# Attention followed by two mixers on one core: input splits moved to the values' copies, both X operands of a head in one tile, fewer transfers to fill it

## The chip, the cores and the metric

The kernel runs on one core of one Trainium2 chip. TensorE (PE in the profile) multiplies, VectorE (DVE), ScalarE (ACT) and GpSimd (POOL) work on elements, and SyncE (SP) issues most of the DMA transfers. Each engine works its own queue of instructions in order. The metric is the device time of one execution in microseconds (us). Three runs of the kernel before took 878.94, 878.44 and 873.46 us, a median of 878.44 us.

## The reference

Three stages run one after the other on 4 sequences of 576 positions and 512 channels:

```python
scores = scale * q @ k^T                       # 4 x 8 heads, 576 x 64
bias = -(cum[:, None] - cum[None, :])          # cum: running sum of max(s, 0)
scores = where(causal, -1e9, scores + min(bias, 0))
attn = softmax(scores) ; x = attn @ v          # heads side by side: 576 x 512
xk, xr = mu * x + (1 - mu) * x_prev            # x_prev: one position earlier
k = max(xk @ w_k, 0) ; y = sigmoid(xr @ w_r) * (k * k @ w_v)
u = y + (max(y^T @ w_tok1, 0) @ w_tok2)^T      # mixes positions
out = u + max(u @ w_ch1, 0) @ w_ch2            # mixes channels
```

All of it is in 32-bit floats. The kernel keeps that precision by writing most operands as a sum hi + lo of two values of TensorE's faster format (fp32r) and multiplying hi by hi, hi by lo and lo by hi.

## The kernel before

**Attention.** The 8 heads of sequence 0 are computed first, with plain 32-bit products (`early` for the first 256 positions, `late` for the rest). The 24 heads of sequences 1 to 3 follow, and each is called a *visit*, 0 to 23. A visit's scores are computed in row blocks j = 0 to 3 of 128 rows. The last 64 rows of an even visit and of the odd one behind it share a block j = 4, which stands in the even visit, so that this block already needs the operands of the odd visit. `scores` (L303) multiplies for each block: L317 takes the tile X1 (4 rows with the bias, and hi of q and k on partitions 64 to 127), L318 the tile X2 (lo of q with hi of k on partitions 0 to 63, hi of q with lo of k on 64 to 127). VectorE finds the row maximum (L288), ScalarE exponentiates (L299), GpSimd divides by the sum (L302). `transposes` turns the block, and `values` (L475) multiplies by V in two column parts c = 0 and 1 per visit. At its end ScalarE copies half of the result out of the accumulator into the tile `tmp` (L503, 48 copies in all), and VectorE adds the other half to it (L506).

**Where X1 and X2 come from.** q and k of two heads (an even and an odd visit) are split in four *splits*, 48 in all and numbered s = 0 to 47. `split` (L235): ScalarE rounds the raw piece to hi (L75, tile PB), GpSimd subtracts to get lo (L242), SyncE writes both to the buffer `hl_d` in the chip's memory (L243) and loads the raw piece of split s + 3 (L232). The place for hi and lo is double, so split s needs the write of split s - 2 to have landed. Splits 4m to 4m + 3 belong to visits 2m and 2m + 1. `place` (L270) then fills X1 and X2 of one visit with four transfers: the bias rows (L276) and three pieces of `hl_d` (L277 to L279). There are two sets of X tiles, so the fill of visit i waits until the last product of visit i - 2 is done (for even visits: of the block j = 4 of visit i - 2). `load_v` (L252) fetches V of two heads into the tile VS with three transfers, `split_v` makes hi and lo of it.

**The mixers.** Products of the first mixer (`h`, `r`, `vd`, all L108) of the sequence before are interleaved with the attention, the second mixer comes after it.

**What sets the order.** The code is recorded in blocks with places (`with at(...)`), and a scheduler with its own model of the durations makes the fixed order of each engine's queue from them. `split_at` gives the splits their places; since a split depends on nothing but its raw piece and the double place, the scheduler is free to draw it forward. All the transfers spoken of here stand in SyncE's one queue: a transfer that waits there holds up those behind it.

## Time and profile before

| | |
|---|---|
| runs | 878.94, 878.44, 873.46 us |
| profiled execution, its own time | 876.96 us |
| its span, first to last instruction | 874.9 us |
| mean granted clock of TensorE | 0.984 |
| busy share | PE 97%, DVE 55%, ACT 52%, POOL 39% |
| moved by DMA | 108.34 MB |

The span is what the trace shows; 2.06 us of the execution lie outside it. The busy share is an average over the span. A table by stretches of time tells which engine limits a stretch, a table of waits tells what ended the idle time of an engine, and the granted clock, 1.00 or 0.50 of full speed, tells how fast TensorE worked in a stretch: 1.00 is its level of 2.4 GHz, 0.50 that of 1.2 GHz.

### The profile page before, as it was taken

What the parts mean: (1) busy time and instruction counts of PE and PEld (TensorE: products, weight loads), DVE (VectorE), ACT (ScalarE), POOL (GpSimd) and SP (SyncE); (2) the same over time, 40 slices, a digit from 0 to 9 for tenths busy, and PEclk for the clock granted to TensorE, in tenths of its full rate; (3) what the DMA queues carried; (4) which work ended last, traced back from release to release, by engine and by line L of the source; (5) the groups of instructions that cost most, each with busy time, mean ns of one, the idle gap of its engine ahead of it and who ended that gap; (6) DMA issues with size and microseconds to landing.
All of it is one profiled execution on the core that took longest, in us unless ns stands there. A gap on an engine that the chain in (4) does not pass through costs nothing. (4 is left out here: it accounts for less than half of the span.)

```text
span 874.9 us, 17429 instructions
## 1 busy us (share of the span) xinstructions
PE 847.9 (97%) x6125; PEld 794.3 (91%) x6125; DVE 484.6 (55%) x1351; ACT 453.5 (52%) x1256; POOL 339.6 (39%) x600
## 2 busy tenths in 40 slices
PE   7999999989799999999999999999999999999998
PEld 5756767989699999999999889999999999999998
DVE  4877775565879566985469756961331222222221
ACT  3988866865785756868377864840310211211210
POOL 3664766765785534645257844720000000000000
PEclk7989999999999999999999999999999999999999
DMA  7953598689963344431234645562022112112100
GB/s 186 255 154 92 168 254 233 183 244 248 239 183 86 91 113 114 99 97 37 82 97 137 219 141 194 181 197 90 10 85 60 41 34 73 37 37 70 41 25 25
DMA packets 88023, 108.34 MB, mean 124 GB/s; under 512 B 11152, under 2 KB 71568, under 8 KB 87936
## 3 DMA queue, kind: packets, MB, share of 16 engines
q1 hardware_dynamic: 81408, 91.56, 37.6%
q0 software_dynamic: 4576, 15.08, 5.4%
q8 instruction: 48, 0.79, 0.4%
q10 hardware_dynamic: 1952, 0.60, 0.4%
q14 instruction: 39, 0.32, 0.1%
HBM read 77.74 MB, written 28.90 MB: 122 GB/s over the span
## 5 line engine op out<-in xcount | busy, mean ns | idle before, releaser
L862 ACT ACTIVATE HID<-c 128x256 fp32r<-128x256 f32 (+1 forms) x96 | 39.3, 409 | 220.7 <-PE c L108 220.6
L108 PE MATMUL vd<-KK,WV 128*128 128x256 f32 (+1 forms) x768 | 123.4, 304 | 0.1
L108 PEld LDWEIGHTS vd<-KK,WV 128*128 128x128 f32 x768 | 109.3, 192 | 3.4 <-issue 1.1
L302 POOL TENSOR_SCALAR P<-P,sum 128x128 f32<-128x128 f32 (+4 forms) x148 | 92.9, 631 | 40.6 <-DVE sum L301 34.8
L108 PE MATMUL h<-XK,WK 128*128 128x320 f32 (+1 forms) x672 | 106.1, 303 | 2.0 <-ACT k L533 1.7
L108 PE MATMUL c<-HID,WV 128*128 128x256 f32 (+1 forms) x768 | 104.8, 291 | 0.0
L108 PE MATMUL c<-U,WK 128*128 128x256 f32 (+1 forms) x768 | 103.2, 291 | 1.3 <-DVE HID L863 1.3
L108 PEld LDWEIGHTS c<-HID,WV 128*128 128x128 f32 x768 | 100.6, 188 | 0.0
L108 PEld LDWEIGHTS c<-U,WK 128*128 128x128 f32 x768 | 98.6, 188 | 1.6 <-DVE HID L863 1.6
L299 ACT ACTIVATE P<-P,mx 128x128 f32<-128x128 f32 (+4 forms) x148 | 86.6, 586 | 23.7 <-DVE mx L288 22.8
L108 PEld LDWEIGHTS h<-XK,WK 128*128 128x128 f32 x672 | 94.2, 190 | 3.8 <-ACT k L533 2.2
L863 DVE SCALAR_TENSOR_TENSOR HID<-c,HID 128x256 fp32r<-128x256 f32 (+1 forms) x96 | 43.8, 456 | 81.1 <-ACT HID L862 81.0
L288 DVE CUSTOM_DVE_ANT_0 P<-s,maskc 128x128 f32<-128x128 f32 (+4 forms) x148 | 72.1, 498 | 28.2 <-PE t L442 15.1
L927 DVE TENSOR_TENSOR ut<-c,ut 128x256 f32<-128x256 f32 (+1 forms) x32 | 14.6, 458 | 119.0 <-PE c L108 108.1
L108 PE MATMUL r<-XR,WR 128*128 128x320 f32 (+1 forms) x384 | 63.3, 305 | 0.0
L536 POOL TENSOR_TENSOR KK<-k,KK 128x256 fp32r<-128x256 f32 (+1 forms) x64 | 56.9, 893 | 14.8 <-ACT k L535 13.7
L300 POOL TENSOR_SCALAR sum<-sum 128x1 f32<-128x1 f32 (+1 forms) x148 | 31.6, 214 | 77.4 <-ACT P L299 70.1
L108 PEld LDWEIGHTS r<-XR,WR 128*128 128x128 f32 x384 | 54.1, 190 | 1.3 <-ACT k L535 0.2
L108 PE MATMUL c<-HID,WR 128*128 128x256 f32 (+1 forms) x384 | 54.8, 291 | 0.0
L108 PE MATMUL c<-U,C1A 128*128 128x256 f32 (+1 forms) x384 | 52.8, 296 | 0.0
L318 PE MATMUL s<-X 128*128 128x128 f32 (+3 forms) x144 | 45.8, 323 | 6.2 <-DMA X<-hl_d 6.2
L108 PEld LDWEIGHTS c<-U,C1A 128*128 128x128 f32 x384 | 51.5, 190 | 0.2 <-ACT U L912 0.2
(130 smaller groups left out, 1661.4 us busy)
## 6 DMA issues: line engine op xcount, KB each, us to landing
X<-hl_d SPq DMA_DIRECT2D x72, 288.0 KB
hl_d<-PB SPq DMA_DIRECT2D x48, 288.0 KB
raw<-in_moe_w_ch_dram POOLq DMA_DIRECT2D x48, 256.0 KB, 3.4
PB<-in_qk_dram SPq DMA_DIRECT2D x48, 144.0 KB
yt<-y_d SPq DMA_DIRECT2D x16, 288.0 KB
u_d<-yt SPq DMA_DIRECT2D x16, 288.0 KB
raw<-in_moe_w_k_dram SPq DMA_DIRECT2D x8, 512.0 KB
raw<-in_moe_w_v_dram SPq DMA_DIRECT2D x16, 256.0 KB
```

The lines of the kernel that those rows point to most:

```text
L108: nc.tensor.matmul(ps, a, b, start=first and i == 0, stop=last and i == n - 1)
L288: nc.vector.tensor_tensor_reduce(out=P[0:m, c0:c1], in0=ps[0:m, 0:c1 - c0], in1=mask[0:m], scale=-scale, scalar=3.0e38 if x == 0 else mx[0 ...
L299: nc.scalar.activation(out=P[0:m, 0:w], in_=P[0:m, 0:w], func=AF.Exp, bias=mx[0:m, x:x + 1], scale=-1.0, accum_out=sm[0:m, 0:1])
L300: nc.gpsimd.tensor_scalar(out=sm[0:m, 0:1], in0=sm[0:m, 0:1], scalar1=1e-9, scalar2=1.0, op0=ALU.add, op1=ALU.mult)
L302: nc.gpsimd.tensor_scalar(out=P[0:m, 0:w], in0=P[0:m, 0:w], scalar1=sm[0:m, 1:2], scalar2=1.0, op0=ALU.mult, op1=ALU.mult)
L318: nc.tensor.matmul(ps[0:n, 0:c1 - c0], x2[:, 0, a:a + n], x2[:, 1, c0:c1], start=False, stop=True)
L536: nc.gpsimd.tensor_tensor(out=kk[:, 1, m, 0:n], in0=t[:, 0:n], in1=f32(kk[:, 0, m, 0:n]), op=ALU.subtract)
L862: nc.scalar.activation(out=hi, in_=ps, func=AF.Relu)
L863: nc.vector.scalar_tensor_tensor(out=lo, in0=ps, scalar=0.0, in1=f32(hi), op0=ALU.max, op1=ALU.subtract)
L927: nc.vector.tensor_tensor(out=t, in0=ps, in1=t, op=ALU.add)
```

## The change

1. X1 and X2 of a visit become one tile XX of four rows of 576: rows 2 and 3 are X1, rows 1 and 0 are X2. The order of hi and lo in `hl_d` is changed, so that all of partitions 64 to 127 comes in one transfer and the rest of X2 in another: three transfers with the bias rows instead of four, of the same bytes in all. The heads of sequence 0 use the same two tiles, two heads in each, and `late_load` loads two heads together. The rows of zeros of the second tile are written when visit 0 begins, no longer before.
2. Splits 0 to 10 keep places of their own in the table, items 13 to 23. Each later split s = 2i + c + 11 is recorded in `values(i, c)`, behind the copy and the sum, and the copy goes into the split's own place in PB instead of `tmp`. So a split from 11 on can't be finished before that copy and sum, and the copy can't begin before the write of split s - 2 has landed.
3. The last 64 positions of V, which are wanted twice, come in one transfer instead of two, and the load of V moves from block 1 to block 3 of the odd visit.

```diff
-    def x_tile(slot, dtype=F32):
-        return qk_p.tile([128, 2 * S], dtype, tag=f"X{slot}", name=f"X{slot}").rearrange("p (t s) -> p t s", t=2)
+    XX = {}
+
+    def x_tile(x, dtype=F32):
+        return qk_p.tile([128, 4, S], dtype, tag=f"XX{x}", name=f"XX{x}")
+
+    def x_pair(x):
+        XX[x] = x_tile(x, F32R)
+        nc.gpsimd.memset(f32(XX[x][0:64, 2:4]), 0.0)
...
     def xs(i):
-        return X1[i % 2], X2[i % 2]
+        x = XX[i % 2]
+        return x[:, 2:4], (x[:, 1], x[:, 0])
...
     RAW = 3
+    LEAD = 11
+
+    def split_place(s):
+        o = RAW * S // 2 + s % 2 * S
+        return stage()[:, o:o + S]
...
-        o = RAW * S // 2 + s % 2 * S
-        e = stage()[:, o:o + S].rearrange("p (t s) -> p t s", t=2)
-        copy("A", e[:, 1].bitcast(F32R), t)
-        nc.gpsimd.tensor_tensor(out=e[:, 0], in0=t, in1=e[:, 1], op=ALU.subtract)
-        nc.sync.dma_start(out=hl_d[g:g + 2, :, 2 * x:2 * x + 2, c0:c1].rearrange("h d t s -> (h d) t s"), in_=e)
+        e = split_place(s).rearrange("p (t s) -> p t s", t=2)
+        hi, lo = (e[:, 0], e[:, 1]) if x == 0 else (e[:, 1], e[:, 0])
+        copy("A", hi.bitcast(F32R), t)
+        nc.gpsimd.tensor_tensor(out=lo, in0=t, in1=hi, op=ALU.subtract)
+        o = 1 - x
+        nc.sync.dma_start(out=hl_d[g:g + 2, :, o:o + 3:2, c0:c1].rearrange("h d t s -> (h d) t s"), in_=e)
         if s + RAW < 2 * len(visits):
             load(s + RAW)
...
-        for r in (0, TAIL):
-            nc.sync.dma_start(out=VS[r:r + TAIL, n], in_=v[b, 128 * n:S, h * D:(h + 2) * D])
+        tail = v[b, 128 * n:S, h * D:(h + 2) * D]
+        twice = bass.AP(tensor=tail.tensor, offset=tail.offset, ap=[[0, 2], *tail.ap])
+        nc.sync.dma_start(out=VS[:, n], in_=twice)
...
-        if i < 2:
-            X2[i] = x_tile(2 + i, F32R)
-        x1, x2 = xs(i)
-        nc.sync.dma_start(out=f32(x1[0:4]), in_=ext_d[g])
-        nc.sync.dma_start(out=f32(x1[64:128]), in_=t[:, 1:4:2])
-        nc.sync.dma_start(out=f32(x2[0:64]), in_=t[:, 0:4:3])
-        nc.sync.dma_start(out=f32(x2[64:128]), in_=t[:, 1:3])
+        both = bass.AP(tensor=t.tensor, offset=t.offset, ap=[[4 * S, D], [S, 2], [1, 2 * S]])
+        x = f32(XX[i % 2])
+        nc.sync.dma_start(out=x[0:4, 2:4], in_=ext_d[g])
+        nc.sync.dma_start(out=x[64:128].rearrange("p (x t) s -> p x (t s)", x=2), in_=both)
+        nc.sync.dma_start(out=x[0:64, 0:2], in_=t[:, 2:4])
...
                 nc.tensor.matmul(ps[0:n, 0:c1 - c0], x1[:, 0, a:a + n], x1[:, 1, c0:c1], start=True, stop=False)
-                nc.tensor.matmul(ps[0:n, 0:c1 - c0], x2[:, 0, a:a + n], x2[:, 1, c0:c1], start=False, stop=True)
+                nc.tensor.matmul(ps[0:n, 0:c1 - c0], x2[0][:, a:a + n], x2[1][:, c0:c1], start=False, stop=True)
...
-        x = late_x[h] = x_tile(h % 4)
+        if h % 2 == 0:
+            late_x[h + 1] = x_tile(h // 2 % 2)
+        x = late_x[h] = late_x[h + 1 - h % 2][:, h % 2 * 2:h % 2 * 2 + 2]
         nc.sync.dma_start(out=x[0:D], in_=qk[h])
         nc.sync.dma_start(out=x[D:D + 4], in_=ext_d[h])
...
-        tmp = v_p.tile([128, CM], F32, tag="tmp", name="tmp")
+        s = 2 * i + c + LEAD
+        tmp = split_place(s)
         nc.scalar.activation(out=tmp[a, 0:n], in_=ps[z, :], func=AF.Copy)
         cols = [(0, n, base)] if c == 0 or e else [(0, TAIL, S - TAIL), (TAIL, n, base)]
         for c0, c1, q in cols:
             nc.vector.tensor_tensor(out=x[a, 1 + q:1 + q + c1 - c0], in0=ps[a, c0:c1], in1=tmp[a, c0:c1], op=ALU.add)
+        if s < 2 * len(visits):
+            split(s)
...
-    for y in range(2 * len(visits)):
-        n = 15 + y if y < 4 else N1 + PER // 4 * (y // 4) + 2 * (y % 4) - (13 if y < 8 else 14)
+    for y in range(LEAD):
+        n = 24 - LEAD + y
         split_at.setdefault(n, []).append(y)
...
-            if j == 2 and 0 < h and h + 3 < H:
+            if j == 2 and h % 2 == 0 and 0 < h and h + 3 < H:
                 with at(N0 + n):
+                    late_load(h + 2)
                     late_load(h + 3)
...
-                    for x in range(2):
-                        X1[x] = x_tile(x, F32R)
-                        nc.gpsimd.memset(f32(X1[x][0:64]), 0.0)
+                    x_pair(0)
             if h == H - 1 and j == 2:
                 with at(N0 + n):
...
@@ -691,13 +707,16 @@
         js = visits[i][1]
         if j == 0 and i + 1 < len(visits):
             with at(N0 + n):
+                if i == 0:
+                    x_pair(1)
                 place(i + 1)
         pieces(n)
         if i % 2 and j == 1 and i + 1 < len(visits):
             with at(N0 + n + 0.2):
                 split_v(i + 1)
-                if i + 3 < len(visits):
-                    load_v(i + 3)
+        if i % 2 and j == 3 and i + 3 < len(visits):
+            with at(N0 + n + 0.2):
+                load_v(i + 3)
...
+        both = x_tile(1)
         for y in (4, 6):
-            t = x_tile(y // 2).rearrange("p t s -> p (t s)")
-            early_at.append((t, y, 2))
+            early_at.append((both[:, y - 4:y - 2].rearrange("p t s -> p (t s)"), y, 2))
             early_load(y)
```

Three places of the queues, before and now. X0 and X2 are the tiles of even visits before, XX0 that now; PB is the place of the splits, hl_d the buffer in memory, y_d takes the first mixer's output.

SyncE at the fill of visit 8 (its transfers end each piece), before:

```order
L565 DMA y_d_75<-e_2572 128x320
L243 DMA hl_d_74<-PB_1219 128x2x288
L232 DMA PB_1219<-in_qk_dram 128x288
L276 DMA X0_1477<-ext_d_73 4x1152
L277 DMA X0_1477<-hl_d_74 64x2x576
L278 DMA X2_1582<-hl_d_74 64x2x576
L279 DMA X2_1582<-hl_d_74 64x1152
```

and now:

```order
L582 DMA y_d_75<-e_2731 128x320
L289 DMA XX0_1479<-ext_d_73 4x1152
L256 DMA hl_d_74<-PB_1212 256x1x288
L244 DMA PB_1212<-in_qk_dram 128x288
L290 DMA XX0_1479<-hl_d_74 64x2x1152
L291 DMA XX0_1479<-hl_d_74 64x1152
```

The write of a split (it is split 20) and a raw load now stand between the bias rows and the two large pieces of the fill; before they stood ahead of it.

SyncE at the fill of visit 10, before:

```order
L257 DMA VS_101<-in_v_dram 64x128 x2
L243 DMA hl_d_74<-PB_1219 128x2x288
L232 DMA PB_1219<-in_qk_dram 128x288
L243 DMA hl_d_74<-PB_1219 128x2x288
L232 DMA PB_1219<-in_qk_dram 128x288
L243 DMA hl_d_74<-PB_1219 128x2x288
L232 DMA PB_1219<-in_qk_dram 128x288
L276 DMA X0_1477<-ext_d_73 4x1152
L277 DMA X0_1477<-hl_d_74 64x2x576
L278 DMA X2_1582<-hl_d_74 64x2x576
L279 DMA X2_1582<-hl_d_74 64x1152
```

and now:

```order
L271 DMA VS_101<-in_v_dram 128x1x128
L256 DMA hl_d_74<-PB_1212 256x1x288
L244 DMA PB_1212<-in_qk_dram 128x288
L256 DMA hl_d_74<-PB_1212 256x1x288
L244 DMA PB_1212<-in_qk_dram 128x288
L289 DMA XX0_1479<-ext_d_73 4x1152
L290 DMA XX0_1479<-hl_d_74 64x2x1152
L291 DMA XX0_1479<-hl_d_74 64x1152
```

Before, the writes ahead of the fill were splits of much later visits. Now the last write ahead of it is split 23, which is a part of visits 10 and 11 themselves, so that the fill needs it.

ScalarE around the copies of the values of visit 5, both parts, and visit 6, part 0 (tmp or PB from pv), before:

```order
L503 ACTIVATE tmp_2606<-pv_2601 64x256
L75 ACTIVATE PB_1219<-PB_1219 128x288
L451 ACTIVATE PF_2722<-t_2703 128x384
L299 ACTIVATE P4_2807,sum_2821<-P4_2807,mx_2808 128x576
L523 ACTIVATE XK_677<-t_2954 128x256
L299 ACTIVATE P0_2857,sum_2863<-P0_2857,mx_2858 128x128
L299 ACTIVATE P1_2900,sum_2906<-P1_2900,mx_2901 128x256
L75 ACTIVATE PB_1219<-PB_1219 128x288
L470 ACTIVATE PT0_1814<-t_2761 128x3x128
L299 ACTIVATE P2_2924,sum_2930<-P2_2924,mx_2925 128x384
L503 ACTIVATE tmp_2671<-pv_2661 64x320
```

and now:

```order
L518 ACTIVATE PB_1212<-pv_2643 64x320
L311 ACTIVATE P0_2838,sum_2844<-P0_2838,mx_2839 128x128
L484 ACTIVATE PT0_1818<-t_2744 128x3x128
L311 ACTIVATE P1_2874,sum_2880<-P1_2874,mx_2875 128x256
L540 ACTIVATE XK_674<-t_2931 128x256
L484 ACTIVATE PT0_1818<-t_2761 128x4x128
L75 ACTIVATE PB_1212<-PB_1212 128x288
L311 ACTIVATE P2_2901,sum_2907<-P2_2901,mx_2902 128x384
L75 ACTIVATE PB_1212<-PB_1212 128x288
L311 ACTIVATE P3_2938,sum_2944<-P3_2938,mx_2939 128x512
L518 ACTIVATE PB_1212<-pv_2707 64x256
```

Now the copy of part 1 of visit 5 goes into the place of split 22 and the next one, of part 0 of visit 6, into that of split 23. The two roundings (L75) between them are those of split 23 (the first: its hi lies where that copy does not write) and of split 22.

## Rows read from the trace of the kernel before

**Rows 1.** The page's part 1: busy us (share of the span), xinstructions.

```profile
PE 847.9 (97%) x6125; PEld 794.3 (91%) x6125; DVE 484.6 (55%) x1351; ACT 453.5 (52%) x1256; POOL 339.6 (39%) x600
```

**Rows 2.** Stretches A:B, us, busy of each engine, then PEclk, DMA share, GB/s.

```profile
126.00:256.00 130.00, 118.17 (x801) 107.62 (x801) 86.02 (x290) 93.58 (x267) 90.80 (x166) 0.97 0.83 225
256.00:430.00 174.00, 173.93 (x1320) 170.77 (x1320) 125.89 (x386) 119.37 (x324) 86.20 (x166) 1.00 0.33 86
```

**Rows 3.** Waits of PE, 126 to 260 us: us in total, times, longest.

```profile
PE s L318 <- DMA X<-hl_d: 6.2, 4, 1.8
...
PE s L317 <- DVE mx L288: 1.4, 4, 0.5
```

**Rows 4.** Timeline of PE: start, us, instruction, [idle before <-what ended it].

```profile
146.39 0.45 PE L318 MATMUL s<-X 128*128 128x128 f32 x1 [1.45 <-DMA X<-hl_d]
...
193.89 0.30 PE L318 MATMUL s<-X 128*128 128x128 f32 x1 [1.81 <-DMA X<-hl_d]
...
217.41 0.30 PE L318 MATMUL s<-X 128*128 128x128 f32 x1 [1.32 <-DMA X<-hl_d]
...
235.04 0.33 PE L318 MATMUL s<-X 128*128 128x128 f32 x1 [1.65 <-DMA X<-hl_d]
```

**Rows 5.** Stretches as in Rows 2, behind the first of these waits.

```profile
146.40:149.70 3.30, 3.30 (x14) 3.26 (x15) 1.33 (x5) 2.11 (x5) 3.10 (x6) 0.50 1.11 257
```

**Rows 6.** DMA issues by line, part 6 of the page: xcount, KB of each.

```profile
X<-hl_d SPq DMA_DIRECT2D x72, 288.0 KB
hl_d<-PB SPq DMA_DIRECT2D x48, 288.0 KB
...
PB<-in_qk_dram SPq DMA_DIRECT2D x48, 144.0 KB
```

**Rows 7.** Timeline of SP's queue: first issue of five fills (visits 2, 6, 8, 10; a late one).

```profile
139.49 0.27 SPq L276 DMA_DIRECT2D X<-ext_d  x1
...
186.21 0.35 SPq L276 DMA_DIRECT2D X<-ext_d  x1
...
209.91 0.34 SPq L276 DMA_DIRECT2D X<-ext_d  x1
...
228.11 0.30 SPq L276 DMA_DIRECT2D X<-ext_d  x1
...
355.71 0.27 SPq L276 DMA_DIRECT2D X<-ext_d  x1
```

**Rows 8.** Stretches as in Rows 2, at the fill that begins at 355.71 us.

```profile
360.50:361.50 1.00, 1.00 (x9) 0.99 (x8) 0.75 (x3) 0.95 (x3) 0.83 (x3) 1.00 0.47 97
361.50:362.00 0.50, 0.50 (x5) 0.42 (x4) 0.50 (x1) 0.50 (x2) 0.50 (x2) 1.00 0.00 0
```

**Rows 9.** Tile PB, 126 to 256 us (busy ACT, POOL); then its writes as a line.

```profile
126.00:256.00 130.00, 16.61 (x38) 31.07 (x38) 0.97 0.83 225
...
L243 SPq DMA_DIRECT2D hl_d<-PB x48: 359/375/535, 94.7 to 256.1; - x48
```

**Rows 10.** Waits of ACT, 85 to 260 us: us in total, times, longest.

```profile
ACT PB L75 <- DMA hl_d<-PB: 19.2, 16, 3.1
```

**Rows 11.** Lines L503 and L506, 126 to 256 us; L503, 205 to 245 us.

```profile
L503 ACT ACTIVATE tmp<-pv x19: 375/383/437, 143.8 to 252.4; 64x256 f32<-64x256 f32 x10, 64x320 f32<-64x320 f32 x9
...
L506 DVE TENSOR_TENSOR xt<-pv,tmp x24: 197/408/498, 145.4 to 253.6; 64x256 f32<-64x256 f32 x15, 64x64 f32<-64x64 f32 x5, 64x320 f32<-64x320 f32 x4
...
L503 ACT ACTIVATE tmp<-pv x8: 376/404/435, 206.0 to 239.3; 64x320 f32<-64x320 f32 x4, 64x256 f32<-64x256 f32 x4
```

**Rows 12.** Timeline: a write of a split, and the ACT rounding that waited for it.

```profile
130.18 0.41 SPq L243 DMA_DIRECT2D hl_d<-PB  x1
...
134.48 0.45 ACT L75 ACTIVATE PB<-PB 128x288 fp32r<-128x288 f32 x1 [2.64 <-DMA hl_d<-PB]
```

**Rows 13.** Timeline of ACT: the copy of visit 6, part 0.

```profile
222.19 0.38 ACT L503 ACTIVATE tmp<-pv 64x256 f32<-64x256 f32 x1
```

**Rows 14.** Zero rows of X, both tiles, ns min/median/max.

```profile
L680 POOL MEMSET X<- x2: 1061/1062/1064, 87.6 to 100.3; 64x1152 f32 x2
```

## The prediction

> **What bounds the kernel now.** I read the page's part 1 first: TensorE is busy for 847.9 us, 97% of the span [rows 1], so only its idle time and the time it spends at half clock can be won; the change takes no product away. Then the stretches [rows 2]: from 126 to 256 us, visits 1 to 11, PE works 118.17 of 130 us, so 11.83 us are idle, the granted clock is 0.97 in the mean, and the DMA engines are 0.83 busy at 225 GB/s. From 256 to 430 us PE is idle for 0.07 us and the DMA share is 0.33. So everything that this change can win lies before 256 us. Third, what PE waited for there [rows 3]: 6.2 us in four waits for the tiles that fills bring, 1.4 us for row maxima; the rest are gaps that no wait explains, and I leave them. Fourth, the four waits themselves [rows 4], always in front of L318, the second product of a block, so X2 was late and X1 was not. Last, the clock: right behind the first of them the granted clock is 0.50, the level of 1.2 GHz, for about 3.3 us [rows 5], after PE had stood still for 1.45 us. The mean of 0.97 over 130 us lacks 0.03 x 130 = 3.9 us of full clock; as rounded it may be 3.3 to 4.6, so I take two such stretches, behind the waits of visits 2 and 6, which cost half of their length each, 3.4 us together (estimate from rows 2 and 5).
>
> **Why the fills are late.** A fill's time is the end of the wait [rows 4] less its first issue [rows 7]: 6.90, 7.68, 7.50 and 6.93 us for visits 2, 6, 8 and 10. PE was ready (start less wait) 5.45, 5.87, 6.18 and 5.28 us after that issue. A lone fill, issued at 355.71 us [rows 7], ends near 361.3: in 360.5 to 361.5 the DMA share is 0.47, afterwards 0 [rows 8]. So 5.6 us for 864 KB (three times 288, rows 6), bias rows apart. The fills lose 1.3 to 2.1 us to other transfers, largely splits: 38 of the 48 are made between 126 and 256 us [rows 9], 432 KB each [rows 6].
>
> **Part by part, against 876.96 us.**
>
> Paced splits. The copies that carry them are 19 in that stretch [rows 11], so some 19 splits move behind 256 us, 19 x 432 KB = 8.2 MB of the 29 MB that 225 GB/s make in 130 us; about 160 GB/s are left. Behind 256 us they cost ScalarE 0.44 us each (16.61/38) and GpSimd 0.82 (31.07/38) [rows 9], where these engines are busy for 119 and 86 of 174 us [rows 2]: nothing, with at most 19 x 0.82 us of GpSimd's work as price were that slack gone.
>
> Visit 2: a fill of 5.6 us against a PE that is ready at 5.45 leaves a wait of 0.15 for 1.45: -1.30 (bounds -1.45 and 0). Visit 6: 5.6 against 5.87, wait gone: -1.81 (bounds -1.81 and 0).
>
> Visit 8: a split's write and a raw load now stand between the bias rows and the large pieces (SyncE's rows in the change). They add 432 KB at 225 GB/s, 1.9 us, and two issues of about 0.4 [rows 12]: 5.6 + 1.9 + 0.8 = 8.3 us against 6.18, a wait of 2.1 for 1.32: +0.8. Bounds: -1.32 if they hide beside the fill, +3 if the write must itself wait for GpSimd there.
>
> Visit 10: the fill now needs split 23, whose hi and lo come behind the copy of visit 6, part 0, at 222.19 us [rows 13]. From there: copy 0.38, sum 0.41 [rows 11], rounding beside them, GpSimd 0.82, issue and landing 3.9 (the write issued at 130.18 ended the wait of the rounding at 134.48, less 0.41 of it as issue: rows 12). That is 0.38 + 0.41 + 0.82 + 0.41 + 3.9 = 5.9 us, so 228.1, which is when this fill was issued before. The large pieces take 5.3 to 5.6 behind it and PE is ready at 233.39: a wait of 0 if no queue waits, of 5 if ScalarE or GpSimd are behind by one other piece of work each. I take the middle, 2.5 for 1.65: +0.9 (bounds -1.65, +3.4).
>
> Clock: without the waits of visits 2 and 6 nothing lets the clock fall there: -3.4. Bounds -3.4 and 0: other waits may fell it.
>
> ScalarE's new wait. A copy into a split's place needs the write of the split before last. Behind the copy stand the exponentials of the next block, for which GpSimd, the transposes and at last PE wait. Before, only roundings waited for such writes, 19.2 us in 16 waits, 1.2 in the mean and 3.1 at most [rows 10], and PE did not care. The copies lie 4.75 us apart (eight from 206.0 to 239.3, rows 11), so the write two back was begun 9.5 us earlier; its chain of 5.9 us ends well before that. I take one of these waits reaching PE, +1.2 (bounds 0, and 8 x 3.1 if all copies between visits 6 and 10 meet the longest).
>
> At nothing, together: one issue less for a fill, whose end its bytes set (at most -0.6 each); one issue less for V and its load two blocks later, since its VS is wanted a visit on; `tmp`'s buffers; the rounding that waits for VectorE's sum, 0.41 us [rows 11], in three of four splits, hidden by the 4.75 us; two heads of sequence 0 in one tile, whose loads run ahead of their use; the second tile's zeros, 1.06 us on GpSimd [rows 14], now at the start of visit 0 (at most +1.1, if its division is what PE waits for).
>
> Merged pieces: all of partitions 64 to 127 comes in one transfer of 576 KB, so the first product, L317, starts later than it did with X1 alone. In all four waits L317 had run and L318 stood [rows 4], and with the merge both would stand: one more product idle, 0.30 us, for each visit that still waits, here 8 and 10, +0.6 at most; I take 0 of it, since the end of the whole fill is what counts. Against the merge also speaks the Trainium skill, "Perfetto Trace Analysis", section "DMA Optimizations": splitting transfers into smaller chunks lets some start sooner when the DMA engines are mostly idle. By it the sum would be 0.6 higher; but 0.83 of DMA busy in this stretch is not idle.
>
> Sum: 876.96 - 1.30 - 1.81 + 0.8 + 0.9 - 3.4 + 1.2 = 873.4. The profiled execution lies 1.48 under the median of the runs and within them (873.46 to 878.94), so I leave it there: **873.5 us**.
>
> **The rivals.** *All fills come in time* (A). If the freed DMA share also hides the extra split at visit 8 and split 23 is written early, all four waits go, with the clock's stretches and the waits for row maxima: 876.96 - 6.2 - 3.4 - 1.4 = 866.0. For it: 0.33 of DMA share is what the stretch behind 256 us gets by with. Against: in visits 8 and 10 SyncE's order is now worse for the fill.
>
> *ScalarE is held by the splits' writes* (B), slower. The chain of one place is copy, sum, rounding, division into lo, issue, landing: 5.9 + 0.44 = 6.3 us, 3.2 for each split, as there are two places. Behind a fill in SyncE's queue a write lands later by the fill's bytes, 864 KB at 225 GB/s or 3.9 us, so 10.2 us for two splits, 5.1 each; the copies are 4.75 us apart. That is the point from which it decides: a write that regularly stands behind a fill or a load makes the copy late, and the exponentials with it. Then eight copies of visits 6 to 10 lose 1.2 us each, 9.6, and visits 2 and 6 still win 3.1, 8 and 10 lose 1.7, the clock stays at its two stretches: 876.96 + 9.6 - 3.1 + 1.7 = 885.2; at 2 us each it is 891.6. For it: SyncE's one queue. Against: a visit has one fill and two copies, so that not every write meets one.
>
> *The waits move, their number stays* (C). Visits 2 and 6 win 3.1, visits 8 and 10 take the same and the clock falls behind these: 877.0.
>
> **How the numbers follow.** Forecast 0.50, A 0.22, B 0.18, C 0.10. About 1% is what a measurement of this kernel can tell from no change, 869.7 and 887.2 around the median. Faster by more: A but for 0.02, and 0.07 of the forecast, whose terms reach 868 if visit 10 waits for nothing and ScalarE's wait stays off PE: 0.27. Slower by more: 0.11 of B and 0.02 of the forecast with both upper bounds at visits 8 and 10: 0.13. Within: 0.60. The range: A's end less 1 us, 865, to B's first price, 885, and 1 for the runs' spread, 886; left out are some 0.08 below and 0.11 above. The forecast's own range is 869 to 878.
>
> **What would show it.** Right: between 126 and 256 us the DMA rate near 160 GB/s, PB's roundings about 19 instead of 38; no wait of PE for XX in visits 2 and 6 and no granted clock of 0.50 there; waits of about 2 us in visits 8 and 10, the one of 10 behind the landing of split 23. ScalarE's copies waiting for hl_d less than five times and PE after them once. Wrong: PE waiting for P tiles or transposes in visits 6 to 11 with ScalarE's copies held by hl_d (B); no wait for XX at all (A); as many dry or half-clock microseconds in other visits (C); idle time of PE behind 256 us, where I take the later splits to cost nothing.

## The result, and the profile after

| | us, median (lowest to highest, runs) |
|---|---|
| kernel before | 875.34 (873.46 to 878.94, 6) |
| changed kernel | 886.98 (882.27 to 887.38, 6) |
| ratio | 1.0114, 95% interval 1.0083 to 1.0146 |

The change made the kernel slower by 1.1%, where 873.5 us was forecast; 886.98 also lies outside the range of 865 to 886. The profiled execution of the changed kernel took 882.27 us, 5.31 more than that of before; it is the shortest of the six, so the traces show about half of the difference of the medians.

First part 1 of its page, then both kernels by stretches (columns as in [rows 2]), those of before first where [rows 2] doesn't have them:

```profile
PE 848.2 (96%) x6125; PEld 795.4 (90%) x6125; DVE 486.2 (55%) x1351; ACT 452.8 (51%) x1256; POOL 338.1 (38%) x600
```

```profile
0.00:60.00 60.00, 53.16 (x279) 36.97 (x280) 42.94 (x138) 41.94 (x106) 31.75 (x77) 0.89 0.80 208
...
430.00:874.90 444.90, 436.59 (x3345) 432.89 (x3344) 182.11 (x407) 150.33 (x422) 90.74 (x129) 1.00 0.30 92
```

```profile
0.00:60.00 60.00, 51.61 (x273) 36.92 (x274) 42.55 (x136) 41.44 (x106) 31.52 (x77) 0.89 0.78 208
...
126.00:256.00 130.00, 119.01 (x803) 109.17 (x802) 83.32 (x282) 86.15 (x244) 76.77 (x149) 0.96 0.67 171
256.00:430.00 174.00, 170.47 (x1287) 166.09 (x1286) 124.74 (x382) 122.65 (x339) 99.49 (x184) 1.00 0.51 132
...
430.00:880.50 450.50, 441.10 (x3395) 438.08 (x3393) 184.57 (x415) 153.38 (x428) 90.74 (x129) 1.00 0.30 91
```

TensorE's busy time is the same (848.2 for 847.9 us), so all of the loss is idle time: stretch less busy time is 8.39 us after for 6.84 before ahead of 60 us, 10.99 for 11.83 from 126 to 256, 3.53 for 0.07 from 256 to 430, 9.40 for 8.31 at the end. The stretch that the change aims at gained 0.84 us; the largest loss stands where nothing was dry before. The stretches are the same times and not quite the same work: the first score product of visit 0 stands at 130.1 us now, at 126.1 before.

The pacing did what it says. From 126 to 256 us the DMA rate fell from 225 to 171 GB/s and the share from 0.83 to 0.67, and tile PB is rounded 21 times there instead of 38 [rows 9]:

```profile
L75 ACT ACTIVATE PB<-PB x21: 426/437/452, 128.0 to 254.4; 128x288 fp32r<-128x288 f32 x21
```

Yet the waits for the fills are still there. The timeline of PE after, the waits of over 0.7 us from visit 2 to 430 us but for two of 0.95 and 0.92 behind VectorE (L329 and L330 are L317 and L318 of before; XX is the tile of a fill):

```profile
147.94 0.30 PE L329 MATMUL s<-XX 128*128 128x128 f32 x1 [1.36 <-DVE mx L300]
149.09 0.33 PE L330 MATMUL s<-XX 128*128 128x128 f32 x1 [0.85 <-DMA XX<-hl_d]
...
217.85 0.41 PE L329 MATMUL s<-XX 128*128 128x128 f32 x1 [1.89 <-DVE xt L521]
...
235.66 0.33 PE L330 MATMUL s<-XX 128*128 128x128 f32 x1 [1.08 <-DVE VV L77]
...
237.91 0.50 PE L108 MATMUL h<-XK,WK 128*128 128x256 f32 x2 [1.23 <-ACT XK L540]
...
243.36 2.74 PE L108 MATMUL h<-XK,WK 128*128 128x256 f32 x21 [1.20 <-ACT k L550]
...
294.18 0.30 PE L329 MATMUL s<-XX 128*128 128x128 f32 x1 [1.91 <-issue]
```

Visit 2 waits 2.21 us instead of 1.45 [rows 4], now in front of both products. Visit 6 waits no more. Visit 8 waits 1.89, visit 10 1.08, visit 14 (294.18) 1.91, where there was no wait. In four of these rows the view names another releaser. It is not the cause: the scores read nothing that the sum L521 or the cast L77 writes, and by the records of PE's sequencer the wait for XX ends at 147.89, 217.79 and 294.12 us, and the fill that the product at 235.66 needs lands at 235.61. Two waits are of the other kind: `h` stood behind ScalarE, and ScalarE behind the write of a split. The timeline of ACT, and its waits from 126 to 260 us as a line, where before no copy waited for such a write [rows 10]:

```profile
185.51 0.43 ACT L518 ACTIVATE PB<-pv 64x320 f32<-64x320 f32 x1 [2.84 <-DMA hl_d<-PB]
...
236.99 0.43 ACT L518 ACTIVATE PB<-pv 64x320 f32<-64x320 f32 x1 [2.16 <-DMA hl_d<-PB]
```

```profile
ACT PB L518 <- DMA hl_d<-PB: 5.0, 2, 2.8
```

A third copy, at 242.18, waited 2.32 us. The view names PE there, but the write issued at 234.94 had only landed at 242.08, and the sequencer's record ends the copy's wait for hl_d behind that; PE's 1.20 us at 243.36 follow. Before, PE had stood at this place too, once, and ScalarE had waited 0.99 us for such a write (at 237.65) ahead of that `k`:

```profile
240.19 1.08 PE L108 MATMUL h<-XK,WK 128*128 128x256 f32 x7 [1.68 <-ACT k L533]
```

Half clock between 126 us and the last products, 3.41 us each: before at 146.34, 194.13 and 511.57 us, after at 149.62, 217.89 and 238.37, each behind an idle PE. Three stretches became three.

### The profile page after: what moved, and what is told of

The parts are those of the page before. It is cut to its first block, busy times and chain, and to the rows that moved or that the text cites. A ratio compares the mean times of both kernels' runs of the same rounds, so it can differ in the third digit from the quotient of the medians.

```text
span 880.5 us, 17418 instructions
## 1 busy us (share of the span) xinstructions
PE 848.2 (96%) x6125; PEld 795.4 (90%) x6125; DVE 486.2 (55%) x1351; ACT 452.8 (51%) x1256; POOL 338.1 (38%) x600
## 4 chain that ended last, share of the span: by engine, by line
PE 74%; DVE 8%; DMA 6%; ACT 5%; issue 3%; POOL 3%; SPq 0%; POOLq 0%; DVEq 0%; ACTq 0%
PE c L108 33%; PE h L108 8%; PE vd L108 7%; PE r L108 4%; PE pv L514 3%; PE t L456 3%; PE t L108 3%; DMA raw<-in_moe_w_ch_dram 2%; PE pv L442 2%; PE s L413 2%; PE s L330 2%; PE s L329 2%; DMA XX<-hl_d 1%; PE idle L168 1%; DVE raw L640 1%
## 5 line engine op out<-in xcount | busy, mean ns | idle before, releaser
L108 PE MATMUL h<-XK,WK 128*128 128x320 f32 (+1 forms) x672 | 108.0, 306 | 2.6 <-ACT XK L540 1.2
L108 PEld LDWEIGHTS vd<-KK,WV 128*128 128x128 f32 x768 | 107.4, 188 | 3.2 <-issue 1.6
L314 POOL TENSOR_SCALAR P<-P,sum 128x128 f32<-128x128 f32 (+4 forms) x148 | 90.3, 613 | 41.9 <-DVE sum L313 32.7
L329 PE MATMUL s<-XX 128*128 128x128 f32 (+3 forms) x144 | 47.0, 333 | 5.9 <-issue 1.9
```

The source lines that it names most:

```text
L108: nc.tensor.matmul(ps, a, b, start=first and i == 0, stop=last and i == n - 1)
L314: nc.gpsimd.tensor_scalar(out=P[0:m, 0:w], in0=P[0:m, 0:w], scalar1=sm[0:m, 1:2], scalar2=1.0, op0=ALU.mult, op1=ALU.mult)
L329: nc.tensor.matmul(ps[0:n, 0:c1 - c0], x1[:, 0, a:a + n], x1[:, 1, c0:c1], start=True, stop=False)
```

## The experiments

Each run stands beside runs of the kernel before on the same chip. Ratios with 95% intervals:

| run | us (lowest to highest) | ratio |
|---|---|---|
| after_again | 884.77 (883.76 to 886.71) | 1.012 (1.0089 to 1.0151) |
| own_tmp | 885.62 (884.18 to 888.13) | 1.0125 (1.0095 to 1.0155) |
| fills_joined | 887.09 (884.75 to 888.51) | 1.0136 (1.0105 to 1.0167) |
| v_behind | 883.93 (878.96 to 888.2) | 1.0099 (1.0067 to 1.0132) |
| old_new_order | 881.43 (874.71 to 883.44) | 1.0058 (1.0025 to 1.0091) |
| change_old_order | 879.09 (877.61 to 882.65) | 1.0049 (1.0026 to 1.0072) |
| paced_old_order | 877.86 (874.36 to 880.83) | 1.0027 (1.0 to 1.0054) |
| tiles_old_order | 888.1 (884.02 to 890.1) | 1.0139 (1.0083 to 1.0194) |
| before_hold | 875.93 (873.56 to 877.75) | 0.9999 (0.9977 to 1.0022) |
| paced_hold | 881.82 (880.1 to 883.11) | 1.0079 (1.0049 to 1.0109) |
| four_new_order | 880.43 (876.91 to 883.97) | 1.0068 (1.0041 to 1.0096) |
| change_four_old_order | 874.31 (869.47 to 876.86) | 0.9995 (0.9976 to 1.0014) |
| three_places | 876.91 (874.84 to 878.57) | 1.0005 (0.999 to 1.0021) |
| three_places_merged | 881.26 (878.46 to 887.65) | 1.0072 (1.0045 to 1.0099) |
| three_places_old | 884.12 (879.48 to 888.63) | 1.0102 (1.0073 to 1.0131) |
| early_old_order | 885.68 (880.64 to 888.95) | 1.0113 (1.0062 to 1.0164) |
| before_x2_in_one | 1042.72 (1041.54 to 1043.84) | 1.1916 (1.1864 to 1.1968) |
| x2_in_one | 1052.86 (1049.85 to 1057.13) | 1.2031 (1.1975 to 1.2088) |

A scheduler orders the queues anew for every edit, so most kernels take their order from a list: the order of each queue of another kernel, given without any wait.

```diff
+    for queue in ORDER:
+        for a, b in zip(queue, queue[1:]):
+            tc.add_manual_dep(b, a.name, NoSync, reason="order")
```

**The changed kernel again**, with no edit, as the measure of the others.

> The changed kernel once more, unchanged, as the yardstick for the runs beside it and for a second trace. Both theories: 885 to 887 us as before. What the second trace is for: the first profiled execution took 882.3 us, 5 us less than most of the timed ones, so it should show which waits vary: either more waiting for XX (transfers), or the same waits and longer ones on ScalarE's copies.

Measured: 884.77; the loss is there in every run. In its trace the waits for XX of visits 2, 8 and 14 are there again (2.45, 1.70 and 1.42 us), the one of visit 10 is not.

**The copy in a tile of its own**, every queue in the changed kernel's order.

```diff
-        tmp = split_place(s)
+        tmp = v_p.tile([128, CM], F32, tag="tmp", name="tmp")
```

> Every queue keeps the order of the changed kernel, instruction by instruction; only the values' copy goes into a tile of its own again and not into the split's place, so that it no longer waits for the write of the split before last. Theory 1 (ScalarE is held by the splits' writes, rival B of the prediction): the waits of 2.84 us at 185.5 and 2.16 us at 237.0 go, with them PE's 1.23 us at 237.9 and the half-clock stretch behind it (1.7 us): 3 to 5 us less than the changed kernel. Theory 2 (the fills are late because of what else stands in SyncE's queue; the copies cost little): at most 1 to 2 us less, and the waits for XX in visits 2, 8 and 14 stay.

Measured: 885.62, no gain. The copy is free, but the rounding right behind it in ScalarE's queue writes the same place and waits in its stead: 3.49 us at 242.85, and PE 3.41 us for `k` at 243.75. So the copy alone is not what holds ScalarE.

**The order of SyncE's transfers**: in the first kernel the three transfers of a fill stand together from visit 2 on, in the second the load of V stands behind the next fill. The fences show the queue, not code.

```diff
- XX<-ext_d, hl_d<-PB, PB<-in_qk, XX<-hl_d, XX<-hl_d
+ XX<-ext_d, XX<-hl_d, XX<-hl_d, hl_d<-PB, PB<-in_qk
```

> The order of the changed kernel in all queues but SyncE's: from visit 2 on the three transfers of a fill stand together, and what stood between them (the write of a split and a raw load at visit 8, V's load at others) behind them. Theory 2: the wait of 1.89 us for XX at 217.9 goes to 0.3 or less with its half-clock stretch (1.7 us), the one of 1.91 us at 294.2 falls by a half or more: 3.5 to 5.5 us less than the changed kernel. Theory 1: these waits stay, within 1 us of it.

```diff
- VS<-in_v, VS<-in_v, XX<-ext_d, XX<-hl_d, XX<-hl_d
+ XX<-ext_d, XX<-hl_d, XX<-hl_d, VS<-in_v, VS<-in_v
```

> The order of the changed kernel in all queues but SyncE's: where V's load stands just ahead of a fill, it stands behind it. Visit 2 is the case: V's load (320 KB) lies between the fills of visits 2 and 3, and goes behind the second. Theory 2: the fill of visit 2 lands some 1.5 us earlier (320 KB at 215 GB/s), its wait of 2.2 us falls to 0.7, and the clock may not fall there: 1.5 to 3.2 us less than the changed kernel. A rival within it: the fill of visit 3 then starts 1.2 us earlier and takes the place of V's bytes, so that the wait stays as it is, within 0.5 us. Theory 1: no change.

Measured: 887.09 and 883.93. Joined, the waits of visit 8 fell to 0.46 us and that of visit 14 went, but PE then waited 3.23 us at 369.74 for ScalarE's `k`, and others: the waits moved. With V behind, visit 2 still waited 0.91 and 0.78, and PE 2.58 us for ScalarE at 247.86. Neither order pays.

**The change taken apart.** Four kernels: the old program in the new order; the whole change in the old order (of its instructions those that are not new); pacing alone, in the old order; the merged tiles and transfers alone, with the old splits and the old order. In words, for the last three (for the first it is the other way round):

```diff
- ORDER = order of the changed kernel
+ ORDER = order of the kernel before
```

> The kernel before, with its own tile for the copies, its four transfers for a fill and its separate tiles, but every instruction that both kernels have stands in the queues where the changed kernel has it (the splits too). Nothing of the change is in it but the order. Theory 3 (the change itself costs and wins little; the scheduler, given other splits and tiles, made another order of all queues, and that order is the slower one): 883 to 887 us. Theory 4 (the copies that pace the splits, the shared tiles or the larger transfers cost the time): 874 to 878 us, as the kernel before.

> The whole change (paced splits in the copies' places, one tile for X1 and X2, three transfers for a fill, one for V's tail), with all other instructions held in the order of the kernel before; only what the change moves by its nature is left to the scheduler: the splits, the zeros, the loads of the heads of sequence 0 and the fills of visits 0 and 1. Theory 3: 870 to 877 us, at best the 873.5 that the prediction's sum gave, since that sum took the other queues as they were. Theory 4: 882 to 888 us.

> The kernel before with the paced splits alone (its tiles, its four transfers, its loads of V), everything but the splits held in the order of the kernel before. Theory 3: 871 to 877 us; the forecast's terms for visits 2 and 6 (3.1 us and the clock's 3.4) less those for visits 8 and 10 (1.7) and 1.2 for ScalarE give 4.6 less at best. Theory 4 with the copies as its cause: 880 us or more.

> The other half: the kernel before with one tile for X1 and X2, three transfers for a fill and one for V's tail, the splits where they were before and the copies in their own tile; all in the order of the kernel before but for the loads of the heads of sequence 0, the zeros and the fills of visits 0 and 1. Theory 3: 874 to 878 us, no change. Theory 4 with the shared tiles or the merged transfers as its cause: 880 us or more.

Measured: 881.43, 879.09, 877.86 and 888.1. No part gains. Pacing alone lowers the DMA rate to 174 GB/s and still waits for X 7.7 us in four waits before 256, where the kernel before has 6.2 [rows 3]:

```profile
126.00:256.00 130.00, 118.17 (x829) 108.66 (x828) 89.02 (x300) 90.55 (x261) 80.58 (x157) 0.99 0.68 174
```

```profile
PE s L337 <- DMA X<-hl_d: 7.7, 4, 2.8
```

The fills of visits 6 and 8 do take 0.4 us less (7.24 and 7.11 us for 7.68 and 7.50), but PE is ready for them that much earlier. So it isn't mainly the splits that make the fills late. The merge alone is the worst of the four, 12.8 us; what pacing does there is to make up for part of the merge.

**The next fill held back.** A last suspicion was that the next transfers (V's load, the odd visit's fill), which follow at once, slow the even visit's fill. Here they wait until it has landed, in the kernel before and in pacing alone.

```diff
+    for late, i in HELD:
+        for y in (1, 2, 3):
+            tc.add_manual_dep(by_tag[late], by_tag["x", i, y].name, Sync, reason="hold")
```

> The kernel before, order and all, with the same hold. Theory 5: three of its four waits (1.45, 1.81, 1.32, 1.65 us) fall below 0.5 although all splits are still there: 869 to 873 us. The prediction's premise (the splits make the fills late): the waits stay within 0.3 of what they were: 874 to 877 us, or more where the held fill is late.

> paced_old_order with one thing more: from visit 3 on, the fill of an odd visit (and V's load where it stands between) may not begin before the fill of the even visit ahead of it has landed. Theory 5 (the fills of even visits are late because V's load and the next fill, 320 and 864 KB, share the DMA engines with their last third; the splits have little to do with it): in paced_old_order the five waits for X in visits 2, 6, 8, 10 and 12 are 1.76, 1.73, 1.40, 2.81 and 2.94 us, 10.6 together, with no split's write issued beside the first of these fills; with the hold those of visits 2, 6 and 8 fall below 0.5, the other two below 1.5: 869 to 874 us. Rival: a fill takes its 7 us whatever stands behind it, or the held fill is then late for the block j = 4: 877 to 882 us.

Measured: 875.93 (nothing) and 881.82 (slower). That theory fell too, but the run shows a fill by itself. Pacing alone, held, visit 2: SyncE's timeline, PE's, and the stretches around its end:

```profile
140.76 0.27 SPq L295 DMA_DIRECT2D X<-ext_d  x1
141.08 0.55 SPq L296 DMA_DIRECT2D X<-hl_d  x1
141.72 0.61 SPq L297 DMA_DIRECT2D X<-hl_d  x1
142.38 0.60 SPq L298 DMA_DIRECT2D X<-hl_d  x1
147.55 0.39 SPq L274 DMA_DIRECT2D VS<-in_v_dram  x1
```

```profile
145.57 0.33 PE L336 MATMUL s<-X 128*128 128x128 f32 x1
147.53 0.33 PE L337 MATMUL s<-X 128*128 128x128 f32 x1 [1.63 <-DMA X<-hl_d]
```

```profile
146.00:146.50 0.50, 0.00 (x0) 0.00 (x0) 0.50 (x3) 0.50 (x2) 0.00 (x0) 1.00 0.63 129
146.50:147.00 0.50, 0.00 (x0) 0.00 (x0) 0.50 (x3) 0.50 (x3) 0.23 (x1) 1.00 0.02 0
147.00:147.50 0.50, 0.00 (x0) 0.00 (x0) 0.50 (x2) 0.29 (x2) 0.41 (x2) 1.00 0.00 0
```

The DMA share ends at about 146.5, 5.7 us after the first issue. That is how I had read 5.6 us [rows 7, 8]. But PE starts at 147.53, 6.77 us after the issue, with 0.00 of DMA share ahead of it. The share counts a packet in the stretch where it starts; the last packets of the trace end at 146.79, so that some 0.7 us pass between the last byte and the product that waits for it. The Trainium skill, "DMA: Bandwidth & Descriptors", section "Anatomy of one DMA — SWDGE (gpsimd) path", puts most of a transfer's fixed time, about 2 us, into the receipt of the write behind the last byte. It says so of transfers issued by GpSimd, these are SyncE's; that the 0.7 us are such a receipt is not shown.

The lone fill of [rows 7] agrees: its last transfer landed at 362.27, 6.56 us after its first issue, by its semaphore's record. Beside other transfers a fill took 0.1 to 0.9 us longer. The fills of visits 2 and 6 before, then this one, from first issue to product:

```profile
139.49:146.39 6.90, 5.11 (x35) 4.29 (x34) 6.90 (x22) 5.18 (x15) 4.83 (x9) 1.00 0.85 217
186.21:193.89 7.68, 5.41 (x38) 4.70 (x36) 6.17 (x25) 5.80 (x18) 5.58 (x13) 1.00 1.00 266
```

```profile
140.76:147.53 6.77, 5.00 (x35) 4.23 (x34) 6.77 (x22) 4.73 (x14) 2.96 (x7) 1.00 0.60 133
```

At 133 GB/s, its own bytes alone, it is 6.77 us; at 217 GB/s in all 6.90, at 266 GB/s 7.68.

**The fill in four transfers again**, X1 first, all else of the change kept: in its own order and in the old one.

```diff
-        nc.sync.dma_start(out=x[64:128].rearrange("p (x t) s -> p x (t s)", x=2), in_=both)
+        nc.sync.dma_start(out=x[64:128, 2:4].rearrange("p t s -> p (t s)"), in_=both[:, 1])
         nc.sync.dma_start(out=x[0:64, 0:2], in_=t[:, 2:4])
+        nc.sync.dma_start(out=x[64:128, 0:2].rearrange("p t s -> p (t s)"), in_=both[:, 0])
```

> The changed kernel in its own order, but a fill is four transfers again (the bias rows, X1 on partitions 64 to 127, X2 in two), so that the first product waits for 288 KB and not for 576. Theory 6 (what the change itself costs in its order, 884.8 here against 881.4 for the old program in that order, is the merged transfer): 881 to 882.5 us, the waits of visits 2, 8 and 14 each one product or about 0.7 us shorter. Rival (it is the copies or the tiles): 884 to 887 us.

> change_old_order with four transfers for a fill. Theory 6: 875 to 877.5 us, its waits in front of the first product of visits 2, 4, 6 and 12 (0.84, 0.28, 1.03, 1.03 us) gone or moved to the second product and shorter. Rival: 878 to 880 us, as change_old_order.

Measured: 880.43 for the 884.77 of three transfers, and 874.31 for 879.09 in the old order, where the ranges don't meet: the merge costs 4.3 and 4.8 us. In both pairs PE, ScalarE, VectorE and GpSimd work through the same queues, instruction by instruction. In the old order the change with four transfers is equal to the kernel before. The waits of PE from 126 to 256 us in the old order, with three transfers and with four:

```profile
PE s L344 <- DMA XX<-hl_d: 2.4, 4, 1.0
...
PE s L345 <- DMA XX<-hl_d: 2.0, 4, 0.9
```

```profile
PE s L346 <- DMA XX<-hl_d: 3.4, 4, 1.7
```

With three, both products of the block stand, with four the second alone. In the new order visit 2's fill goes from first issue to second product in 6.87 us (141.69 to 148.56) with four transfers and in 7.33 (141.76 to 149.09) with three. In these traces PE's waits in front of the scores of visits 2, 8, 10 and 14 and at 348 us sum to 7.9 us with three and 4.7 with four. What comes later is X1. In visit 2 it landed 4.12 us after the fill's first issue with four transfers, and with three, as a part of the 576 KB, after 6.05 (by the semaphores' records). Alone, the whole fill is as fast: the last one of change_old_order, three transfers with nothing beside them, landed after 6.49 us, X1 after 5.52; the lone one of [rows 7], four transfers, after 6.56, X1 after 4.05. Why in visit 2 the whole came later too, no run shows.

What is left in the new order is ScalarE. With four transfers, timelines of SyncE, ACT and PE, then ACT's waits from 126 to 260 us:

```profile
234.63 0.59 SPq L307 DMA_DIRECT2D XX<-hl_d  x1
235.32 0.55 SPq L271 DMA_DIRECT2D hl_d<-PB  x1
```

```profile
241.95 0.38 ACT L534 ACTIVATE PB<-pv 64x256 f32<-64x256 f32 x1 [3.02 <-DMA hl_d<-PB]
```

```profile
243.12 2.29 PE L123 MATMUL h<-XK,WK 128*128 128x256 f32 x9 [2.57 <-ACT k L566]
```

```profile
ACT PB L534 <- DMA hl_d<-PB: 7.5, 3, 3.2
...
ACT PB L90 <- DMA hl_d<-PB: 3.6, 3, 1.9
```

The write was issued right behind a fill and ended the copy's wait 6.63 us later; the write of [rows 12], with no fill ahead of it, did so in 4.30, and in the changed kernel that of split 23, issued at 225.07, had landed in 2.63. Behind the copy `k` was late, PE stood for 2.57 us, and the clock was 0.50 from 241.59 for 6.83 us.

**A third place for hi and lo**, so that a copy needs the write of the split three back; the order of every queue is kept in the first two kernels (four transfers, three transfers). The third kernel is the one of four transfers in the old order, with the splits left to the scheduler.

```diff
-        o = RAW * S // 2 + s % 2 * S
+        if s % 3 == 2:
+            return act["PB3"]
+        o = RAW * S // 2 + s % 3 * S
```

> four_new_order (880.4 us), its order in every queue untouched, with three places for hi and lo instead of two, so that the copy and the rounding of split s wait for the write of split s - 3. Theory 7 (rival B: in the new order ScalarE is held by splits' writes that land late behind a fill): ScalarE's waits for hl_d of 3.23 us at 185, 1.28 at 226 and 3.02 at 242 go, PE's 2.57 us at 243 and the 6.8 us at half clock with them: 874 to 877 us. Rival (the order costs elsewhere, in DVE's and GpSimd's queues): 879 to 882 us.

> The changed kernel in its own order, its merged transfer kept, with the third place. Theory 7: 4 to 6 us less than the 884.8 to 887 of the changed kernel, 879 to 882 us, what is left being the merged transfer. Rival: 884 to 887 us.

> change_four_old_order (874.3 us) with the third place. In that order ScalarE has no wait over 1 us for hl_d near 240 us, so that both theories give little: 872 to 875 us. It is the candidate that could beat the kernel before.

Measured: 876.91 for 880.43, and 881.26 for 884.77: 3.5 us each time, and the merge again costs 4.4. The kernel before has two places as well, so a third takes nothing of the change back: the 3.5 us are what two places cost in this order. ACT's waits from 126 to 260 us in three_places, where one of the six is left:

```profile
ACT PB L538 <- DMA hl_d<-PB: 0.9, 1, 0.9
```

and the stretch around the former wait is full, at full clock; here with four transfers and two places, then with three places:

```profile
241.50:248.50 7.00, 5.38 (x24) 5.38 (x25) 4.84 (x14) 5.71 (x19) 4.10 (x8) 0.51 0.40 126
```

```profile
241.50:248.50 7.00, 7.00 (x56) 6.69 (x55) 6.03 (x17) 5.86 (x20) 5.27 (x9) 1.00 0.46 147
```

The third kernel missed: the splits moved in the queues, and PE waited 7.66 us at 126.07 for ScalarE's transposed block. It says nothing on the places.

**The stage before 126 us in the old order**, four transfers, the rest in the new order; in words:

```diff
- ORDER = new
+ ORDER = old until 126.1 us, new behind it
```

> four_new_order (880.4 us) with every queue in the order of the kernel before as far as that kernel had come when PE began the first visit (126.1 us), and in the new order behind it. If the order's cost lies in the stage of the weights and sequence 0 (the traces lose 2.7 to 3 us more than before between 40 and 80 us, 1.2 to 1.5 between 100 and 120): 876 to 877.5 us. If it lies in the visits: 879 to 882 us.

Measured: 885.68, 5 us worse than without. New waits stood at 51.52 (2.68 us, ScalarE) and around the seam (1.05 at 130.04, 1.97 at 133.55): a miss, which leaves open what the stage before 126 us costs.

**All of X2 in one transfer** of 576 KB over 128 partitions, X1 apart, so that the first product need not wait for the whole; in the change and in the kernel before.

```diff
+        low = bass.AP(tensor=t.tensor, offset=t.offset, ap=[[2 * S, 2], [4 * S, D], [1, 2 * S]])
+        nc.sync.dma_start(out=x[64:128, 2:4], in_=t[:, 1:3])
+        nc.sync.dma_start(out=x[:, 0:2].rearrange("p t s -> p (t s)"), in_=low)
```

> change_four_old_order (874.3 us) with a fill of three transfers cut in another way: the bias rows, X1 (288 KB), and all of X2 in one (576 KB on 128 partitions), so that the first product waits for X1 alone and X2 is issued 0.6 us earlier. If a fill's own length sets the waits (6.8 us from the first issue to PE's start, of which issues are about 2.1): each of the waits for XX shorter by about 0.6, 872 to 874 us. If bytes or other transfers set them: 874 to 876 us.

> The kernel before, in its order, with nothing changed but that X2 is filled by one transfer of 576 KB on 128 partitions instead of two (the rows of hl_d lie as in the changed kernel for that). If a fill's own length sets its four waits for X (1.45, 1.81, 1.32, 1.65 us): each shorter by about 0.6 us, so 2.4 less, and one half-clock stretch may go: 871 to 873.5 us. If not: 874 to 877 us.

Measured: 1052.86 and 1042.72, 19 to 20% slower, a miss that shows something else (last section).

## Why the prediction was wrong, point by point

**The step that failed first is the length of a fill.** I took 5.6 us from the end of the DMA share, set it against a PE that is ready after 5.3 to 6.2 us, and so put the lateness down to the splits beside it. The product can start only some 0.7 us behind the last byte: a fill is 6.77 us with nothing beside it, and was 6.90 in visit 2 before, beside other transfers. Set against the same instants, 6.77 us make 4.3 of the 6.2 us that PE waited; the other 1.9 are what came beside. So a fill is late mostly by its own length and the instant of its issue, which in visit 2 the end of block j = 4 of visit 0 set. So the gains of pacing were never there: visit 2 (-1.30) took +0.76 in the change, and pacing alone took 1.0027 of the time. The step says "5.6 us for 864 KB"; 7 us in its place would have left -0.7 of visit 6 and nothing of visit 2.

**Visit 6** (-1.81): the wait went as said, but not for the reason given. It is gone in the old program in the new order too, and with pacing alone in the old order it stayed, 1.73 us: the order of the queues can take it away, the freed DMA share alone did not.

**Visits 8 and 10** (+0.8, +0.9): the wait of visit 8 was 1.89 for the 2.1 forecast, with the split between the pieces as described, but two errors cancel in it: from first issue to product it was 7.85 us for 8.3, of which a fill is 6.8 and not 5.6, and the split some 1.1 and not 2.7. The fill of visit 10 was issued at 228.25 for the 228.1 worked out from split 23's chain, and that is luck: split 23's write had landed at 227.70, and what the issue waited for was the end of block j = 4 of visit 8, PE's product that ended at 228.28. Its wait was 1.08, and 0.18 in front of the first product, for 2.5. The same pattern stood at visit 14, where I had looked at no fill: 1.91 us, most of the idle time behind 256 us, which I had taken at nothing.

**The merge** ("+0.6 at most; I take 0"): 4.3 to 4.8 us, by three pairs of runs, all with paced splits. Two things were missed. What the first product waits for was a transfer of 288 KB and is now one of 576 KB, and in visit 2 the whole fill ended later, not sooner (7.33 for 6.87 us). And I priced one product of 0.30 us for each visit that waits, where the trace has first products that wait 1.4 and 1.9 us. I had set aside the rule of the Trainium skill, "Perfetto Trace Analysis", section "DMA Optimizations", because the DMA engines were not idle. The page puts that condition on the whole task ending sooner and not on some chunks starting sooner; here two transfers of 288 KB in place of one of 576 paid at a DMA share of 0.67 to 0.69.

**ScalarE's new wait** (+1.2; rival B -> 885.2): three copies waited, 7.3 us in all, and PE stood 1.23 and 1.20 us behind the later two, with a stretch of half clock; taking the wait away by a third place gave back 3.5 us, a tile of its own for the copy nothing. That PE did not care before was wrong for one wait, the 1.68 us at 240.19. B's mechanism was right: a write that stands behind a fill lands late. Its price was too, but at two places and not at eight, and its total was near the result for another sum: the merge's 4.4 and ScalarE's 3.5 us make up 7.9 of the 9.0 that the changed kernel, run again, lost.

**The clock** (-3.4): the stretch of visit 6 went, but new ones came behind the waits of visit 8 and of ScalarE, and the one at 511.57 did not come; busy time, in which half clock shows, is the same within 0.3 us.

**Edits at nothing**: no run has V's one transfer and later load, or the two heads of sequence 0 in one tile, by themselves. three_places has them all and is equal to the kernel before, so that together they cost nothing that a median shows. The trace after has 1.55 us more idle time before 60 us, where PE waits 1.93 us at 57.58 for VectorE's maximum; what of the change moves it there is open.

Also open: the old program in the new order took 881.43, in nine runs from 874.71 to 883.44, while three_places, in the same order, took 876.91. ScalarE waits for writes of splits there too, but only 1.8 us in three waits. Its trace (882.99 us) beside that of three_places (877.40), from the first score product of visit 6 to that of visit 12, the same products:

```profile
198.50:271.00 72.50, 65.48 (x443) 60.34 (x442) 55.13 (x172) 50.96 (x146) 47.77 (x89) 0.91 0.74 191
```

```profile
199.30:266.90 67.60, 61.02 (x444) 56.18 (x442) 54.31 (x171) 50.06 (x146) 47.87 (x87) 0.97 0.75 203
```

The idle time is nearly the same, 7.02 and 6.58 us; the other 4.5 us are busy time, with 13.65 us at half clock against 3.41. So what that run loses there is clock and not waiting; why the clock falls more often in it is open. Open is as well why the merge costs 12.8 us where the splits are not paced (tiles_old_order).

No kernel of these beats the one before: change_four_old_order (0.9995) and three_places (1.0005) are equal to it within their intervals.

## What to carry to other kernels

Measure a load from its first issue to the first instruction that used it when that instruction was waiting, not to the end of its bytes; then ask whether it would be late with nothing beside it, before traffic is taken away for its sake. Merging transfers joins what waited apart: the first consumer now waits for the sum, so the saved issue has to be worth more than that. When a buffer gets a second job, its old wait moves ahead of everything that stands behind the new user in that engine's queue; one more buffer, with the order of the queues kept, tells what that wait costs.

## What the runs showed of the hardware

A transfer of 576 KB whose outermost dimension is 2 took some 15 us. In the kernel before with X2 in one transfer: SyncE's issue, the product that waited for it, and stretches between:

```profile
156.18 0.54 SPq L296 DMA_DIRECT2D X<-hl_d  x1
```

```profile
171.50 0.47 PE L335 MATMUL s<-X 128*128 128x128 f32 x1 [11.16 <-DMA X<-hl_d]
```

```profile
162.00:164.00 2.00, 0.00 (x0) 0.00 (x0) 1.14 (x5) 0.00 (x0) 1.13 (x3) 1.00 0.13 49
164.00:166.00 2.00, 0.00 (x0) 0.00 (x0) 0.00 (x0) 0.00 (x0) 0.00 (x0) 0.66 0.12 51
```

With nothing else to do, the DMA share is 0.12, and 0.12 x 16 engines is 2 engines, at 51 GB/s. The Trainium skill, "DMA: Bandwidth & Descriptors", section "Rules for kernel authors", states this rule: an outermost dimension below 16 confines a transfer to at most so many engines. The trace agrees for 2. The change's transfer of V's tail also has an outermost dimension of 2, at 64 KB; what that costs was not measured by itself, but three_places has it and is equal to the kernel before.
